# Interleaving VectorE's state rows, and taking half of the last skip terms straight from x, in a gated S5 + GELU kernel

## The chip, the cores and the metric
The kernel runs on one core of one Trainium2 chip. The metric is the device time of one execution, in microseconds; smaller is better. The kernel before has a median of 209.35 us over three runs (208.24 to 209.89).

## The reference, cut to what matters
The input x is [2048, 640] in bf16. One branch (a) is a diagonal complex state-space layer with 640 states, one is a dense layer (b) with 1728 hidden units, and a sigmoid gate per row mixes them.

```python
g = sigmoid((x * gate_w).sum(-1, keepdims=True))
Lam_bar = exp(dt * Lam)                       # complex, one per state
Bu = einsum("bld,pd->blp", x, B_bar)          # complex
h[t] = Lam_bar * h[t-1] + Bu[t]               # 2048 steps
a = 2 * einsum("blp,dp->bld", h, C).real + x * Dskip
b = gelu(x @ w1 + b1) @ w2 + b2
out = g * a + (1 - g) * b
```

## The kernel before, in words
The 2048 rows of x are cut into 4 chunks of 512 (`NCH`, `CH`), and each chunk into 4 output tiles of 128 rows (`TPC`; tile number `ti`, and `H = 2` tiles make a half). The 640 states are 5 blocks of 128 (`KS`); one block of one chunk is called a **state row** here, so there are 20.

**TensorE** runs these stages in an order written out at the end of the function (L953 to L996): `ff1(c)` (L345, matmuls L305) computes the hidden layer of a chunk, `ssm(c)` (L619, matmuls L481) computes Bu, `fin_b(c)` (L706, matmuls L717) is the second dense product by a seven-product scheme on halves, and the state part of the output is `fin_a(c)` (L784, matmuls L797) for chunks 0 and 1 and `fin_s(c)` (L845, matmuls L857, seven products again) for chunks 2 and 3. The last stages are `fin_b(2)`, `fin_s(2)`, `fin_b(3)`, `fin_s(3)`. All products are made in 8 PSUM banks of 128 x 512 f32 (`bank()`); a product into a bank that is reused waits for the last reader of that bank.

**ScalarE** evicts PSUM: the GELU (L314), Bu into a bf16 tile `bu` (L484), copies of a bank into another one (`fork`, L729 in `fin_b` and L863 in `fin_s`), and the gated outputs of the dense branch into f32 tiles `gb` (`out_of`, L737). `part_7` (L750) writes the product Q into `gq`; an accumulating DMA from GpSimd's queue (`twice`, L703; `plus`, L661) adds it, in both column halves, to another tile.

**VectorE** does the recurrence. For a state row, `scan_ops` (L546) puts nine steps in a list `pend`, each with a time from which it may run, a cost, and a function: `f1` cos product of bu, `f2` sin product of bu, `f3` their sum v (a rotation by the state's angle, so that the recurrence becomes real), `f4` twice a `tensor_tensor_scan` over 512 steps (real and imaginary part; L571), `f5` the carry to the next chunk, `f6`, `f7`, `f8` the rotation back into `hs`. All products go through one function, so that their line is L552. The tiles `wa`, `wb` and `v` have one buffer each, `g` has two, `bu` eight. For chunks 1 and 2, `f5` leaves the carry to four small ScalarE instructions (L585), which read the last column of `g`.

**The order on each engine** is the order in which the program issues instructions. A small clock model (`ck`, L225) decides it: each matmul adds to `ck.pe`, each ScalarE instruction to `ck.act`. `let_out(until)` (L236) issues steps from `pend` as long as the modelled VectorE time is before `until`; `dve_now(ready, cost, fn)` (L246) first lets steps out up to `ready` and then issues `fn`. The model knows nothing of a DMA's landing. Other VectorE work stands between the state rows in this way: the fold of C (L533), the skip products x * Dskip (`skip`, L647), the output evictions (`ot`, L802 and L872), the four sums of `hs` for the seven products (`h_sums`, L824).

**SP's queue** carries the loads and stores in program order: after the last `ff1`, two DMA transposes of `gelN` (L337), a load `gel<-eL` (L343), then the loads of x tiles (`load_xn`, L126).

**The skip term of the last two chunks.** For tiles of chunks 2 and 3, x * Dskip (bf16, `xn`) is multiplied by the gate on ScalarE into an f32 tile `GS[c][a]` (`gated`, L833, instruction L836), for all four tiles of the chunk, and VectorE adds that to `gb` (`skip_in`, L839, instruction L843, which the profile shows as L842). The f32 tiles lie in weights that are no longer used (`wide`, L818 to L820). For tiles 2 and 3 of the chunk, `fin_b` first lets the DMA (`twice(gs[H + j], ...)`) add Q into the same tile.

```python
986  fin_b(2, {1: lambda: (gated(2, H), gated(2, 0), load_xn(NT - TPC), load_xn(NT - TPC + 1)),
987            2: lambda: minus_c(3),
988            3: lambda: skip_in(2, (0, 1), 0, HD)}, GS[2])
990  fin_s(2, lhs, rhs, {0: lambda: skip_in(2, (0, 1), HD, D, ck.act + 0.5), 1: lambda: minus_d(3)})
991  skips(3, H)
992  fin_b(3, {0: lambda: (let_out(1e9), skips(3), [f() for f in last]), 1: lambda: gated(3, H), 2: lambda: gated(3, 0),
993            3: lambda: skip_in(3, (0, 1), 0, HD)}, GS[3])
```

The numbers 0 to 3 are hooks, places in `fin_b` (L753 to L779) and `fin_s`. In `fin_b` hook 1 stands behind the products into Y, hook 2 behind `out_of("X", 1, 1)`, and hook 3 behind `out_of("Z", 1, 0)`, ahead of the last product and `out_of("X", 0, 1)`. So the x tiles of chunk 3 are loaded at L981 (tiles 14 and 15, into `w1c_hi` and `xB`) and at L986 (tiles 12 and 13, into the `xn` pool), their skip products are made at L991 and L992, and they are gated in `fin_b(3)`.

Of the kernel before, what the change touches and what calls it, by code (L numbers as in the profile page):

```python
# [42 lines left out]
def kernel(  # L43
# [80 lines left out]
    def load_xn(ti, dst=None):  # L124
        xn[ti] = xnp.tile([P, D], BF16, name="xn") if dst is None else dst
        nc.sync.dma_start(out=xn[ti][:], in_=x2d[ti * P:(ti + 1) * P, :])  # L126
# [106 lines left out]
    def later(ready, cost, fn, c=-1):  # L233
        pend.append((ready, cost, fn, c))
# [307 lines left out]
    def settle(keep=None):  # L542
        while small and (ck.pe > small[0][0] if keep is None else len(small) > keep):
            small.pop(0)[1]()

    def scan_ops(c, ks, bu, ready):  # L546
        wide = lambda t: t[:, ks:ks + 1, :].to_broadcast([P, 2, CH])
        sines = TSIN2[:, ks, :, :]
        s = {}

        def tt(o, a, b, op):
            nc.vector.tensor_tensor(out=o, in0=a, in1=b, op=op)  # L552

        def f1():
            s["mc"] = work.tile([P, 2, CH], BF16, name="wa", bufs=1)
            tt(s["mc"][:], wide(TCOS), bu[:], ALU.mult)

        def f2():
            s["ms"] = work.tile([P, 2, CH], BF16, name="wb", bufs=1)
            tt(s["ms"][:], sines, bu[:], ALU.mult)  # L560

        def f3():
            s["v"] = work.tile([P, 2, CH], BF16, name="v", bufs=1)
            tt(s["v"][:], s["mc"][:], s["ms"][:, ::-1, :], ALU.add)

        def f4(ri):
# [4 lines left out]
            nc.vector.tensor_tensor_scan(s["g"][:, ri, :], r_c[:, ks:ks + 1].to_broadcast([P, CH]),  # L571
                                         s["v"][:, ri, :], init, ALU.mult, ALU.add)

        def f5():
            g = s["g"]
            if c == 0:
                m = work.tile([P, 2], F32, name="e2")
                end = g[:, :, CH - 1:CH].rearrange("p r o -> p (r o)")
                tt(m[:], end[:, ::-1], sn[:, ks, :], ALU.mult)
                nc.vector.scalar_tensor_tensor(out=carry[:, :, ks], in0=end, scalar=cL[:, ks:ks + 1], in1=m[:], op0=ALU.mult, op1=ALU.add)  # L580
                return

            def turn_carry():
                m = work.tile([P, 2], F32, name="e1")
                one = lambda out, i, sc, b: nc.scalar.activation(out=out, in_=g[:, i, CH - 1:CH], func=ACT.Identity,  # L585
                                                                 scale=sc[:, ks:ks + 1], bias=b)
# [8 lines left out]
        def f6():  # L595
            s["no"] = work.tile([P, 2, CH], BF16, name="wa", bufs=1)
            tt(s["no"][:], wide(TCOS), s["g"][:], ALU.mult)

        def f7():
            s["ns"] = work.tile([P, 2, CH], BF16, name="wb", bufs=1)  # L600
            tt(s["ns"][:], sines, s["g"][:], ALU.mult)

        def f8():
            to = lambda t: t.rearrange("p r (i t) -> p r i t", i=2)
            dst = hs[c][:].rearrange("p i r k t -> p r i k t")[:, :, :, ks, :]
            tt(dst, to(s["no"][:]), to(s["ns"][:, ::-1, :]), ALU.subtract)

        later(ready, 0.68, f1)
        later(0, 0.65, f2)
        later(0, 0.75, f3)  # L610
        later(0, 1.27, lambda: f4(0))
        later(0, 1.21, lambda: f4(1))
        if c < NCH - 1:
            later(0, 0.25 if c == 0 else 0.0, f5)
        later(0, 0.69, f6)
        later(0, 0.62, f7)
        later(0, 0.7, f8, c)

    def ssm(c, at={}, given=()):  # L619
        hs[c] = hsp.tile([P, 2, 2, KS, HT], BF16, name="hs")  # L620
# [82 lines left out]
    def twice(dst, src):  # L703
        plus(dst.rearrange("p (h d) -> p h d", h=2), src[:].rearrange("p (o d) -> p o d", o=1).to_broadcast([P, 2, HD]))

    def fin_b(c, at={}, gs=None):  # L706
# [54 lines left out]
        if c == NCH - 1:  # L761
            part_7()
            for j in range(H):
                twice(gs[H + j], gq[j])
        both("X", N2, TB)
        fork("X", "Z")
        if c < NCH - 1:
            part_7()
        if c == NCH - 2:
            for j in range(H):  # L770
                twice(gs[H + j], gq[j])
        both("X", s1, TA)
        out_of("X", 1, 1)
        hook(2)
# [43 lines left out]
    wide = [narrow(w1a_sb[:], 6 * D)[:, j * 2 * D:(j + 1) * 2 * D].bitcast(F32) for j in range(3)]  # L818
    wide += [xA[:].rearrange("p k t -> p (k t)")[:, KS * HT:].bitcast(F32), narrow(w1c_lo[:], 2 * D).bitcast(F32)]
    GS = {2: [wide[i] for i in (0, 1, 3, 4)], 3: [wide[i] for i in (2, 0, 3, 4)]}  # L820
# [12 lines left out]
    def gated(c, a0):  # L833
        for a in (a0, a0 + 1):
            ti = c * TPC + a
            nc.scalar.activation(out=GS[c][a], in_=xn[ti][:], func=ACT.Identity, scale=gcol[:, 0, ti:ti + 1])  # L836
            act(0.82)

    def skip_in(c, tiles, d0, d1, ready=0):  # L839
        for a in tiles:  # L840
            gb = gbs[c * TPC + a]
            dve_now(ready, 0.82 if d1 - d0 > HD else 0.45, lambda: nc.vector.tensor_tensor(  # L842
                out=gb[:, d0:d1], in0=gb[:, d0:d1], in1=GS[c][a][:, d0:d1], op=ALU.add))  # L843

    def fin_s(c, lhs, rhs, at={}):  # L845
        A = dict(zip((1, 7, 6, 2, 5, 3, 4), lhs))
# [103 lines left out]
    def sums(c):  # L950
# [30 lines left out]
    for j, t in ((0, w1c_hi[:].rearrange("p k f -> p (k f)")[:, 0:D]), (1, xB[:].rearrange("p k t -> p (k t)")[:, KS * HD:KS * HD + D])):  # L981
        load_xn(NT - H + j, t)
# [12 lines left out]
    skip_in(3, (0, 1), HD, D)  # L995
# [31 lines left out]
```

## Time and profile before

| what | us |
|---|---|
| median of three runs | 209.35 (208.24 to 209.89) |
| the profiled execution's own time | 207.85 |
| its span in the trace | 206.1 |
| TensorE busy | 200.8 (97%), 1290 matmuls, granted clock 1.00 |
| VectorE busy | 190.3 (92%), 304 instructions |
| ScalarE busy | 143.3 (70%), 275 instructions |
| GpSimd busy | 50.4 (24%) |
| last matmul of the chain ends | 202.06 |

Times in the trace are counted from the span's start; the execution's own time is 1.75 us more than the span. VectorE and ScalarE instructions overlap at their ends: the next one can start while the one before is still recorded as running. So the price of an instruction in a queue is the distance from its start to the next start, and not its recorded duration. The profile's releaser of a wait is the instruction that ended last among those waited for.

In the chain of work that ended last, TensorE's lines hold 91% of the span and VectorE's 6%; the VectorE part lies between 173.5 and 184.4.

### The profile page before, as it was taken

What the parts mean: (1) busy time and instruction counts of PE and PEld (TensorE: products, weight loads), DVE (VectorE), ACT (ScalarE), POOL (GpSimd) and SP (SyncE); (2) the same over time, 40 slices, a digit from 0 to 9 for tenths busy, and PEclk for the clock granted to TensorE, in tenths of its full rate; (3) what the DMA queues carried; (4) which work ended last, traced back from release to release, by engine and by line L of the source; (5) the groups of instructions that cost most, each with busy time, mean ns of one, the idle gap of its engine ahead of it and who ended that gap; (6) DMA issues with size and microseconds to landing.
All of it is one profiled execution on the core that took longest, in us unless ns stands there. A gap on an engine that the chain in (4) does not pass through costs nothing.

```text
span 206.1 us, 3584 instructions
## 1 busy us (share of the span) xinstructions
PE 200.8 (97%) x1290; PEld 120.6 (59%) x1301; DVE 190.3 (92%) x304; ACT 143.3 (70%) x275; POOL 50.4 (24%) x83
## 2 busy tenths in 40 slices
PE   8999999999999999999999999999999999998993
PEld 5844544454477644675457777544447677776762
DVE  2689998999999999999999999999999999999983
ACT  3598765997876889992574897268866987257720
POOL 8317930313230500031001052200411171014000
PEclk9999999999999999999999999999999999999999
DMA  6989998999999450269923379902676999538303
GB/s 180 206 137 229 204 275 144 199 212 264 207 147 246 109 81 11 65 113 245 197 55 60 67 133 245 238 4 80 106 133 118 167 226 202 125 94 165 61 0 127
DMA packets 45191, 30.28 MB, mean 147 GB/s; under 512 B 26899, under 2 KB 42613, under 8 KB 45173
## 3 DMA queue, kind: packets, MB, share of 16 engines
q0 software_dynamic: 6448, 12.53, 35.8%
q1 hardware_dynamic: 38148, 17.03, 34.8%
q10 hardware_dynamic: 576, 0.49, 0.8%
q8 instruction: 10, 0.16, 0.3%
q14 instruction: 9, 0.07, 0.2%
HBM read 7.79 MB, written 2.62 MB: 51 GB/s over the span
## 4 chain that ended last, share of the span: by engine, by line
PE 91%; DVE 6%; ACT 1%; issue 1%; DVEq 0%
PE bank L305 28%; PE bank L717 22%; PE bank L481 21%; PE bank L797 11%; PE bank L857 6%; DVE ot L872 2%; PE bank L264 1%; PE bank L329 1%; DVE gb L884 1%; DVE gb L842 1%; DVE wb L552 1%; PE bank L267 0%; ACT gq L750 0%; ACT xA L836 0%; ACT w1c_lo L836 0%
## 5 line engine op out<-in xcount | busy, mean ns | idle before, releaser
L314 ACT ACTIVATE gel<-bank,colB 128x512 bf16<-128x512 f32 (+1 forms) x52 | 33.5, 690 | 7.5 <-PE bank L305 7.2
L571 DVE TENSOR_TENSOR_SCAN g<-r_c,carry,v 128x512 bf16<-128x512 f32 x30 | 37.2, 1272 | 0.7
L484 ACT ACTIVATE bu<-bank 128x512 bf16<-128x512 f32 x40 | 23.2, 600 | 18.6 <-PE bank L481 18.5
L717 PEld LDWEIGHTS <-gel 128*128 128x128 bf16 x280 | 27.3, 98 | 11.8 <-issue 1.0
L717 PE MATMUL bank<-w_sb,gel 128*128 128x320 bf16 x168 | 24.1, 299 | 0.0
L305 PEld LDWEIGHTS <-w1a_sb 128*128 128x128 bf16 x162 | 14.7, 103 | 12.0
L737 ACT ACTIVATE gb<-bank,gcol 128x320 f32<-128x320 f32 x32 | 16.0, 524 | 6.5 <-PE bank L717 6.5
L797 PEld LDWEIGHTS <-hs 128*128 128x128 bf16 x160 | 15.6, 98 | 6.0
L481 PEld LDWEIGHTS <-BT_im 128*128 128x128 bf16 x100 | 9.8, 98 | 11.8
L481 PEld LDWEIGHTS <-BT_re 128*128 128x128 bf16 x100 | 9.7, 98 | 11.0
L552 DVE TENSOR_TENSOR wa<-TCOS,bu 128x1024 bf16<-128x1024 bf16 x20 | 13.7, 687 | 1.4 <-DVE hs L552 0.5
L305 PE MATMUL bank<-xA,w1a_sb 128*128 128x128 bf16 (+2 forms) x100 | 14.8, 303 | 0.1
L552 DVE TENSOR_TENSOR v<-wa,wb 128x1024 bf16<-128x1024 bf16 x20 | 13.9, 693 | 0.7
L552 DVE TENSOR_TENSOR hs<-wa,wb 128x1024 bf16<-128x1024 bf16 x20 | 13.8, 690 | 0.6
L552 DVE TENSOR_TENSOR wa<-TCOS,g 128x1024 bf16<-128x1024 bf16 x20 | 13.8, 691 | 0.4
L552 DVE TENSOR_TENSOR wb<-TSIN,bu 128x1024 bf16<-128x1024 bf16 x20 | 13.7, 684 | 0.0
L552 DVE TENSOR_TENSOR wb<-TSIN,g 128x1024 bf16<-128x1024 bf16 x20 | 13.7, 683 | 0.0
L797 PE MATMUL bank<-CT_re,hs 128*128 128x320 bf16 x80 | 13.5, 299 | 0.0
L797 PE MATMUL bank<-CT_im,hs 128*128 128x320 bf16 x80 | 13.5, 299 | 0.0
L717 PEld LDWEIGHTS <-N 128*128 128x128 bf16 x112 | 11.0, 98 | 4.3
L305 PEld LDWEIGHTS <-w1b_sb 128*128 128x128 bf16 x80 | 7.8, 98 | 9.4 <-DMA w1b_sb<-in_B_w_dram 0.2
L729 ACT ACTIVATE bank<-bank 128x320 f32<-128x320 f32 x16 | 6.7, 422 | 9.5 <-PE bank L717 9.3
(189 smaller groups left out, 399.2 us busy)
## 6 DMA issues: line engine op xcount, KB each, us to landing
out_dram<-ot SPq DMA_DIRECT2D x15, 160.0 KB, 3.3
w_sb<-in_B_w_dram SPq DMA_DIRECT2D x4, 480.0 KB, 5.7
gel<-N POOLq DMA_DIRECT2D x4, 448.0 KB, 4.8
xn<-in_A_x_dram SPq DMA_DIRECT2D x10, 160.0 KB, 3.1
N<-gel POOLq DMA_DIRECT2D x3, 448.0 KB, 5.4
gel<-gel POOLq DMA_DIRECT2D x3, 448.0 KB, 7.2
N<-N POOLq DMA_DIRECT2D x3, 448.0 KB, 6.1
gb<-gq POOLq DMA_DIRECT2D x4, 320.0 KB, 4.8
```

Of the source, the lines that this page charges most:

```text
L305: nc.tensor.matmul(p[:, t0:t1], lhsT=w, rhs=xT[c][:, kd, t0:t1], start=(kd == 0) if first is None else first, stop=(kd == last), skip_grou ...
L314: nc.scalar.activation(out=dst, in_=src, func=ACT.Gelu_apprx_tanh, bias=b1_c[p0:p1, kf:kf + 1])
L481: nc.tensor.matmul(p[:], lhsT=BT[ks >= KSA][:, kd, (ks % KSA if ks < KSA else ks - KSA) * P:][:, 0:P], rhs=xT[c][:, kd, :], start=(kd == 0 ...
L484: nc.scalar.activation(out=bu[:, ri, :], in_=p[:], func=ACT.Identity)
L552: nc.vector.tensor_tensor(out=o, in0=a, in1=b, op=op)
L571: nc.vector.tensor_tensor_scan(s["g"][:, ri, :], r_c[:, ks:ks + 1].to_broadcast([P, CH]), s["v"][:, ri, :], init, ALU.mult, ALU.add)
L717: nc.tensor.matmul(p[:, 0:HD], lhsT=lhs[:, s, j * P:(j + 1) * P], rhs=rhs[:, s, :], start=fresh and s == 0, stop=s == KH - 1, skip_group_c ...
L729: nc.scalar.activation(out=quad[j][dst][:, 0:HD], in_=quad[j][src][:, 0:HD], func=ACT.Identity)
L737: nc.scalar.activation(out=gbs[ti][:, h * HD:(h + 1) * HD], in_=quad[j][name][:, 0:HD], func=ACT.Identity, scale=gcol[:, 1, ti:ti + 1])
L797: nc.tensor.matmul(p[:, 0:d1 - d0], lhsT=hs[c][:, a // H, j // KS, j % KS, (a % H) * P:][:, 0:P], rhs=CT[:, j % KS, d0:d1], start=False, s ...
L857: nc.tensor.matmul(t[j][:, d0:d1], lhsT=A[i][:, k, j * P:(j + 1) * P], rhs=B[i][:, k, d0:d1], start=fresh and k == 0, stop=k == KS - 1, sk ...
L872: dve_now(ck.pe + 0.2, 0.54, lambda: nc.vector.scalar_tensor_tensor(out=ots[ti][:, o + d0:o + d1], in0=t[j][:, d0:d1], scalar=gcol[:, 0, t ...
```

## The change
Four edits:

1. `scan_ops` no longer appends a row's nine steps behind the last row's. If steps of the row before are still in `pend`, the new row's steps are woven in: one new step behind the old row's first scan, one behind its carry step, one behind its cos product out, one behind its sin product out, as long as the new row's data is due by the model and more than five of its steps are left. The modelled costs of the steps are changed too.
2. The sin products are made in place, into `bu` and into `g`. The cos product out goes to `wb`, the cos product in to `wa`. For chunks 1 and 2 a VectorE copy of the last column of `g` into a small tile `e3` (four buffers) comes in, and ScalarE's carry reads that.
3. For tiles 0 and 1 of chunks 2 and 3 there is no gated f32 copy any more: `skip_in` computes gate * (x * Dskip) + gb from the bf16 tile in one `scalar_tensor_tensor`. Only tiles 2 and 3 of a chunk keep the copy (`GS` has two tiles per chunk).
4. Order: all four x tiles of chunk 3 are loaded one after the other behind `ff1(3)`, tiles 12 and 13 now into `w1c_lo`. Their skip products move from behind `fin_s(2)` into `fin_b(2)` (hook 1 and hook 2), and `gated(3)` moves from `fin_b(3)` to hook 3 of `fin_b(2)`.

In VectorE's queue this gives, in the last stages: behind the sums for `xA`, the v and the sin product out of two state rows, then the skip products into `w1c_hi` and `xB`, and behind these the rest of the third, the fourth and the fifth state row of chunk 3, the skip products into `w1c_lo`, and the first evictions of `fin_s(2)`. In the kernel before, the two skip products stand behind all evictions of `fin_s(2)`, and the fifth state row behind them. TensorE's order of instructions is the same in both kernels; SP's has the same transfers in the same order, with another target for two of them.

```diff
-        later(ready, 0.68, f1)
-        later(0, 0.65, f2)
-        later(0, 0.75, f3)
-        later(0, 1.27, lambda: f4(0))
-        later(0, 1.21, lambda: f4(1))
...
+        def sin_in():
+            tt(bu[:], sines, bu[:], ALU.mult)
...
+            e = work.tile([P, 2], BF16, name="e3", bufs=4)
+            nc.vector.tensor_copy(out=e[:], in_=end)
...
+        def sin_out():
+            tt(s["g"][:], sines, s["g"][:], ALU.mult)
...
+        new = [(ready, 0.61, cos_in, -1), (0, 0.61, sin_in, -1), (0, 0.61, sum_in, -1), (0, 1.23, lambda: scan(0), -1),
+               (0, 1.21, lambda: scan(1), -1), (0, 0.3 if c == 0 else 0.1 if c < NCH - 1 else 0, ends if c < NCH - 1 else lambda: None, -1),
+               (0, 0.61, cos_out, -1), (0, 0.61, sin_out, -1), (0, 0.63, sum_out, c)]
+        old = latest.ops
+        latest.ops = new
+        left = [x for x in old if x in pend]
+        if not left:
+            pend.extend(new)
+            return
+        k = pend.index(left[0])
+        woven, rest = [], list(pend[k:])
+        t = ck.dve + sum(x[1] for x in pend[:k])
+        at = {3: 1, 5: 1, 6: 1, 7: 1}
+        queue = list(new)
+        for x in rest:
+            woven.append(x)
+            t += x[1]
+            if x in old and old.index(x) in at and queue and t > queue[0][0] - 0.1 and len(queue) > 5:
+                woven.append(queue.pop(0))
+                t += woven[-1][1]
+        pend[k:] = woven + queue
...
-                twice(gs[H + j], gq[j])
+                twice(gs[j], gq[j])
...
+    GS = {2: wide[0:2], 3: wide[2:4]}
...
+    def gated(c):
+        for j in range(H):
+            ti = c * TPC + H + j
+            nc.scalar.activation(out=GS[c][j], in_=xn[ti][:], func=ACT.Identity, scale=gcol[:, 0, ti:ti + 1])
             act(0.82)
...
+            if a >= H:
+                dve_now(ready, 0.82, lambda: nc.vector.tensor_tensor(out=gbs[ti][:], in0=gbs[ti][:], in1=GS[c][a - H], op=ALU.add))
+                continue
+            dve_now(ready, 0.88 if d1 - d0 > HD else 0.48, lambda: nc.vector.scalar_tensor_tensor(
+                out=gbs[ti][:, d0:d1], in0=xn[ti][:, d0:d1], scalar=gcol[:, 0, ti:ti + 1],
+                in1=gbs[ti][:, d0:d1], op0=ALU.mult, op1=ALU.add))
...
+    for a, t in ((H, w1c_hi[:].rearrange("p k f -> p (k f)")[:, 0:D]), (H + 1, xB[:].rearrange("p k t -> p (k t)")[:, KS * HD:KS * HD + D]),
+                 (0, lo[:, 0:D]), (1, lo[:, D:])):
+        load_xn((NCH - 1) * TPC + a, t)
...
-    fin_b(2, {1: lambda: (gated(2, H), gated(2, 0), load_xn(NT - TPC), load_xn(NT - TPC + 1)),
-              2: lambda: minus_c(3),
-              3: lambda: skip_in(2, (0, 1), 0, HD)}, GS[2])
+    fin_b(2, {1: lambda: (gated(2), skips(3, H)),
+              2: lambda: (minus_c(3), skips(3)),
+              3: lambda: (gated(3), skip_in(2, (0, 1), 0, HD))}, GS[2])
...
-    skips(3, H)
-    fin_b(3, {0: lambda: (let_out(1e9), skips(3), [f() for f in last]), 1: lambda: gated(3, H), 2: lambda: gated(3, 0),
+    fin_b(3, {0: lambda: (let_out(1e9), [f() for f in last]),
               3: lambda: skip_in(3, (0, 1), 0, HD)}, GS[3])
```

More of the change, by code (lines that the diff above doesn't have):

```diff
@@ L544, in settle @@
             small.pop(0)[1]()
+    class Row:
+        ops = ()
+    latest = Row()
     def scan_ops(c, ks, bu, ready):
@@ L552, in tt, with cos_in, sum_in, scan @@
             nc.vector.tensor_tensor(out=o, in0=a, in1=b, op=op)
[L554 to L562, printed above, removed]
+        def cos_in():
+            s["w"] = work.tile([P, 2, CH], BF16, name="wa", bufs=1)
+            tt(s["w"][:], wide(TCOS), bu[:], ALU.mult)
+        def sin_in():
+            tt(bu[:], sines, bu[:], ALU.mult)
+        def sum_in():
             s["v"] = work.tile([P, 2, CH], BF16, name="v", bufs=1)
-            tt(s["v"][:], s["mc"][:], s["ms"][:, ::-1, :], ALU.add)
-        def f4(ri):
+            tt(s["v"][:], s["w"][:], bu[:, ::-1, :], ALU.add)
+        def scan(ri):
             if ri == 0:
@@ L572, in f4, with ends @@
                                          s["v"][:, ri, :], init, ALU.mult, ALU.add)
-        def f5():
-            g = s["g"]
+        def ends():
+            end = s["g"][:, :, CH - 1:CH].rearrange("p r o -> p (r o)")
             if c == 0:
                 m = work.tile([P, 2], F32, name="e2")
-                end = g[:, :, CH - 1:CH].rearrange("p r o -> p (r o)")
                 tt(m[:], end[:, ::-1], sn[:, ks, :], ALU.mult)
@@ L581, in f5 @@
                 return
+            e = work.tile([P, 2], BF16, name="e3", bufs=4)
+            nc.vector.tensor_copy(out=e[:], in_=end)
             def turn_carry():
                 m = work.tile([P, 2], F32, name="e1")
-                one = lambda out, i, sc, b: nc.scalar.activation(out=out, in_=g[:, i, CH - 1:CH], func=ACT.Identity,
+                one = lambda out, i, sc, b: nc.scalar.activation(out=out, in_=e[:, i:i + 1], func=ACT.Identity,
                                                                  scale=sc[:, ks:ks + 1], bias=b)
@@ L593, in f5, with cos_out, sum_out @@
             small.append((ck.dve + 2.0, turn_carry))
[L595 to L603, printed above, removed]
+        def cos_out():
+            s["o"] = work.tile([P, 2, CH], BF16, name="wb", bufs=1)
+            tt(s["o"][:], wide(TCOS), s["g"][:], ALU.mult)
+        def sin_out():
+            tt(s["g"][:], sines, s["g"][:], ALU.mult)
+        def sum_out():
             to = lambda t: t.rearrange("p r (i t) -> p r i t", i=2)
             dst = hs[c][:].rearrange("p i r k t -> p r i k t")[:, :, :, ks, :]
-            tt(dst, to(s["no"][:]), to(s["ns"][:, ::-1, :]), ALU.subtract)
-        later(ready, 0.68, f1)
-        later(0, 0.65, f2)
-        later(0, 0.75, f3)
-        later(0, 1.27, lambda: f4(0))
-        later(0, 1.21, lambda: f4(1))
[L613 to L617, printed above, removed]
+            tt(dst, to(s["o"][:]), to(s["g"][:, ::-1, :]), ALU.subtract)
+        new = [(ready, 0.61, cos_in, -1), (0, 0.61, sin_in, -1), (0, 0.61, sum_in, -1), (0, 1.23, lambda: scan(0), -1),
[19 more added lines that the diff above has]
+        pend[k:] = woven + queue
     def ssm(c, at={}, given=()):
@@ L770, in fin_b @@
             for j in range(H):
-                twice(gs[H + j], gq[j])
+                twice(gs[j], gq[j])
         both("X", s1, TA)
@@ L817 @@
     M3 = narrow(xA[:], KS * HT).rearrange("p (k t) -> p k t", k=KS)
-    wide = [narrow(w1a_sb[:], 6 * D)[:, j * 2 * D:(j + 1) * 2 * D].bitcast(F32) for j in range(3)]
-    wide += [xA[:].rearrange("p k t -> p (k t)")[:, KS * HT:].bitcast(F32), narrow(w1c_lo[:], 2 * D).bitcast(F32)]
-    GS = {2: [wide[i] for i in (0, 1, 3, 4)], 3: [wide[i] for i in (2, 0, 3, 4)]}
     C11, C12, C21, C22 = (t[:, :, h * HD:(h + 1) * HD] for t in (CT_re, CT_im) for h in range(2))
@@ L831, in h_sums @@
         return steps, (a, M7, M6, b, g21, M3, d), (C11, U7, U6, C21, U5, C22, U4)
[L833 to L836, printed above, removed]
+    wide = [narrow(w1a_sb[:], 6 * D)[:, j * 2 * D:(j + 1) * 2 * D].bitcast(F32) for j in range(3)]
+    wide.append(xA[:].rearrange("p k t -> p (k t)")[:, KS * HT:].bitcast(F32))
+    GS = {2: wide[0:2], 3: wide[2:4]}
[3 more added lines that the diff above has]
+            nc.scalar.activation(out=GS[c][j], in_=xn[ti][:], func=ACT.Identity, scale=gcol[:, 0, ti:ti + 1])
             act(0.82)
@@ L840, in skip_in @@
         for a in tiles:
-            gb = gbs[c * TPC + a]
-            dve_now(ready, 0.82 if d1 - d0 > HD else 0.45, lambda: nc.vector.tensor_tensor(
-                out=gb[:, d0:d1], in0=gb[:, d0:d1], in1=GS[c][a][:, d0:d1], op=ALU.add))
+            ti = c * TPC + a
+            if a >= H:
[4 more added lines that the diff above has]
+                in1=gbs[ti][:, d0:d1], op0=ALU.mult, op1=ALU.add))
     def fin_s(c, lhs, rhs, at={}):
@@ L980 @@
                10: lambda: (nc.sync.dma_start(out=U4, in_=C21), plus(U4, U6))})
-    for j, t in ((0, w1c_hi[:].rearrange("p k f -> p (k f)")[:, 0:D]), (1, xB[:].rearrange("p k t -> p (k t)")[:, KS * HD:KS * HD + D])):
-        load_xn(NT - H + j, t)
+    lo = narrow(w1c_lo[:], 2 * D)
+    for a, t in ((H, w1c_hi[:].rearrange("p k f -> p (k f)")[:, 0:D]), (H + 1, xB[:].rearrange("p k t -> p (k t)")[:, KS * HD:KS * HD + D]),
+                 (0, lo[:, 0:D]), (1, lo[:, D:])):
+        load_xn((NCH - 1) * TPC + a, t)
     gates(3)
```

## The prediction
> **What bounds the kernel now.** I read the page first, then who waits for whom, then each engine's timeline where a wait ends last. TensorE (PE) is busy for 97% of the span at full clock, and the list of TensorE's waits has one entry behind the start:
>
> ```profile
> PE 200.8 (97%) x1290; PEld 120.6 (59%) x1301; DVE 190.3 (92%) x304; ACT 143.3 (70%) x275; POOL 50.4 (24%) x83
> ```
> ```profile
> PE bank L717 <- ACT bank L729: 0.6, 1, 0.6
> ```
>
> So VectorE (DVE), busy though it is, never holds TensorE up directly in this execution. The one hole shows in TensorE's timeline of `fin_b(3)` (columns: start, duration, engine, line):
>
> ```profile
> 178.83 3.97 PE L717 MATMUL bank<-w_sb,gel 128*128 128x320 bf16 x28
> 182.63 2.06 PE L717 MATMUL bank<-w_sb,N 128*128 128x320 bf16 x14
> 184.53 2.06 PE L717 MATMUL bank<-TB,N 128*128 128x320 bf16 x14
> 187.18 2.06 PE L717 MATMUL bank<-TA,gel 128*128 128x320 bf16 x14 [0.57 <-ACT bank L729]
> ```
>
> Fourteen matmuls take 1.90 from start to start (182.63 to 184.53), so the last line was due at 186.43 and came 0.75 late. Its cause is two steps back, in ScalarE's timeline: the copy (fork, L729) stood behind the gated skip terms, and these waited for VectorE's late skip product:
>
> ```profile
> 184.42 0.83 ACT L836 ACTIVATE xA<-w1c_hi,gcol 128x640 f32<-128x640 bf16 x1 [1.06 <-DVE w1c_hi L647]
> ```
>
> VectorE's prices are read from its timeline, start to next start:
>
> ```profile
> 119.49 2.46 DVE L571 TENSOR_TENSOR_SCAN g<-r_c,carry,v 128x512 bf16<-128x512 f32 x2
> 121.86 1.12 DVE L802 SCALAR_TENSOR_TENSOR ot<-bank,gcol,gb 128x320 bf16<-128x320 f32 x2
> ...
> 124.10 0.55 DVE L802 SCALAR_TENSOR_TENSOR ot<-bank,gcol,gb 128x320 bf16<-128x320 f32 x1
> 124.56 0.68 DVE L552 TENSOR_TENSOR hs<-wa,wb 128x1024 bf16<-128x1024 bf16 x1
> 125.16 0.55 DVE L802 SCALAR_TENSOR_TENSOR ot<-bank,gcol,gb 128x320 bf16<-128x320 f32 x1
> ...
> 163.92 0.69 DVE L552 TENSOR_TENSOR wa<-TCOS,g 128x1024 bf16<-128x1024 bf16 x1
> 164.53 0.68 DVE L552 TENSOR_TENSOR wb<-TSIN,g 128x1024 bf16<-128x1024 bf16 x1
> 165.25 0.69 DVE L552 TENSOR_TENSOR hs<-wa,wb 128x1024 bf16<-128x1024 bf16 x1
> ```
>
> A product followed by independent work takes 0.605 (163.92 to 164.53), one followed by its own reader 0.72. A scan takes 1.19 (two in 2.37), an eviction of 320 columns 0.46. The lines at 124 show that a reader two places behind its writer pays nothing: hs starts 0.46 behind the eviction, though it waits for wb in front of that. Further rows: a skip product 0.40, a plain 320-column add 0.40.
>
> The loads that the change makes urgent stand at the end of SP's queue:
>
> ```profile
> 157.18 3.51 SPq L337 DMA_TRANSPOSE gel<-gelN  x2
> 162.79 0.67 SPq L343 DMA_DIRECT2D gel<-eL  x1
> 163.56 0.54 SPq L126 DMA_DIRECT2D w1c_hi<-in_A_x_dram  x1
> 164.15 0.41 SPq L126 DMA_DIRECT2D xB<-in_A_x_dram  x1
> ```
> ```profile
> w1c_hi<-in_A_x_dram SPq DMA_DIRECT2D x1, 160.0 KB, 2.4
> xB<-in_A_x_dram SPq DMA_DIRECT2D x1, 160.0 KB, 2.3
> ```
>
> L343 waits for the transposes to land and the x tiles queue behind it. They land at 163.56 + 2.4 = 165.96 and 164.15 + 2.3 = 166.45. Nobody felt that before: the skip product read w1c_hi at 183.90.
>
> **The change, part by part.**
>
> Weaving. A row in the old order costs 6.74 (wa at 134.34 to the next wa at 141.08). Woven it is six products at 0.605 and two scans at 1.19, 6.01. Where the e3 copy comes in (ten rows), add a 0.11 wait for the scan and 0.08 for the copy: 6.20. Seventeen rows at about 0.55 are some 9 us off VectorE. On the path that is nothing: TensorE waits for no VectorE work before 178.83. The old evictions in `fin_a` keep up with TensorE, and so do the new ones, whose queue is shorter. Should the cover go, it is 9 us of VectorE.
>
> The Trainium skill speaks against this edit. "VectorE: DVE Perf Modes", section "The DRAIN you can't avoid", says the pipeline empties after every VectorE instruction whatever the semaphores, so that only fewer instructions help, not another order. The rows above (0.605 against 0.72) differ. By that rule the weave would save nothing, and VectorE would come to the w1c_hi product near 169, 9 us later than by the rows, so that the sum below would be 3 us larger.
>
> In place: an in-place bf16 product is in the trace (xn<-xn,Dbc, 483 ns for 640 elements, against 690 for 1024), so no change of price. The e3 copy lies between 0.07 (the gates' 4-element instructions, start to start) and 0.22 (L580); ten of them are 0.7 to 2.2 us, hidden under the 9. ScalarE's carry reads e3 instead of g; its one old wait for g was 0.4 and held nobody. By the sums the copies come before ScalarE asks.
>
> Skip term from x: eight additions of 320 columns get a multiply. Not in the trace from SBUF; bounds are the plain add (0.40) and the eviction's whole duration (0.55); I take 0.46, the eviction's spacing, being the same operation. ScalarE loses four gated products of 0.72. That removes the 0.75 hole, and in `fin_b(2)` another 0.17 (161.45 to 163.52 is 2.07 instead of 1.90). The four accumulating DMAs of GpSimd keep number, size and order; only targets change.
>
> Gating moved: `gated(3)` now stands on ScalarE in front of the last `out_of` of `fin_b(2)`. ScalarE ends the two Z outputs at 168.5, gates until 169.9, evicts X until 170.8, and the first two forks of `fin_s(2)` end at 171.2 and 171.6. TensorE wants them at 171.94 and 172.6. It fits by 0.7; nothing.
>
> Loads of tiles 12 and 13: third and fourth in SP's queue as before (issued at 164.66), without the waits for ScalarE (0.3 and 0.2) that reading `xn` brought. With their 3.4 us they land by 168.6; VectorE's products on them come at 171.0 by the sum below. Nothing.
>
> Skip products moved: the step that decides. They now stand behind `xA` and two products. VectorE comes there about 160.2 (its queue summed with the prices above from the second row on); it can't be earlier than 159.4, since the gates wait for ScalarE's gz at 157.2 and then 0.3 + 0.74 + 1.21 follow. The data lands at 165.96. VectorE is in order, so it stands still for nearly 6 us with three unfinished state rows and the first evictions of `fin_s(2)` queued behind. Those evictions free the bank into which `fin_b(3)` writes first. From the landing on:
>
> - skip into xB at 166.45, next start 166.85
> - 4 scans 4.76, 9 products 5.45, 2 skips 0.80, 4 half additions 1.84, two reader waits 0.22: 13.07, so the eviction starts at 179.91 and ends (0.55) at 180.46. TensorE was due at 178.83: a wait of 1.6
> - the Q product of `fin_b(3)` is due 28 matmuls (3.80) later, at 184.26. Its bank waits for the third pair of evictions: from 179.91 two evictions 0.92, hs 0.61, two evictions 0.92, add to part 7 0.92 (178.26 to 179.18 before), part 7 to eviction 0.98 (179.18 to 180.16), duration 0.55: 184.81. Another 0.55
> - Q at 184.81, X at 186.71, the TA products at 188.61, with no hole now. Before they began at 187.18: 1.43 later.
>
> Behind that nothing new is late: the sums for `fin_s(3)` start near 188 and end near 191.5, the first is read at 195.6. The tail is the same.
>
> **The sum.** 207.85 + 1.43 = 209.3 for the profiled execution, which is 1.5 below the median of the runs and below all of them. I put the step on the median: 209.35 + 1.43 = 210.8.
>
> Unknowns, with both ends: landing 2.1 (the shortest of this line) to 3.4 us (the next two x tiles), -0.2 to +1.1; the half additions -0.2 to +0.4; the queue's length: the same prices over the old queue from 172.81 to 183.90 give 10.55 for 11.09, 5% short, so up to +0.9 in 17.8 us.
>
> **Rivals.**
> - No block: the loads land by 163.6, or the queue is shorter than summed. Then only the holes go: 0.75 + 0.17, 208.4. For it: VectorE saves 9 us. Against: SP's order is unchanged, and the transposes wait for ScalarE's gelN (157.0), which TensorE sets. The gain turns to a loss from a landing at 164.5 on.
> - The landing is later still, the side of clearly slower. If the first two tiles take 3.4 us like the two behind them, they land at 166.96 and 167.55, the queue starts 1.1 later, and all that follows too: 1.43 + 1.1 = 2.5, 211.9. Slower by over 1% (2.1) from a delay of 0.66 on. For it: VectorE's moved work and GpSimd's accumulating DMAs (164.75, 165.49) meet there. Against: these DMAs lie there before too.
> - The weave doesn't do what it says and each product still costs 0.72. VectorE then comes to the skip product near 169, 3 us behind the landing: 1.43 + 3 = 4.4, 213.8. Against: the lines at 124.
>
> **How the numbers follow.** Forecast 0.55, no block 0.18, later landing 0.20, no weaving gain 0.07. About 1% is what a measurement of this kernel tells from no change, here 2.1 us. Slower by over 1%: the later landing, the weave rival less a little, 0.25. Faster by over 1% needs 2.1, and the holes are 0.92 in all: 0.03. Within: 0.72. The range reaches from the no-block case, 208.4, to 1.43 + 1.1 + 0.9 = 3.4 over the median, 212.8. The likeliest case alone is 209.9 to 211.4.
>
> **What would show it.** VectorE idle before the w1c_hi product, released by a DMA, for 5 to 6 us: the block. TensorE waiting for an ot eviction at the start of `fin_b(3)` (1.6) and before Q (0.5): its price. No wait for L729's copy in `fin_b(3)`: the removed hole. Products starting 0.605 apart in woven rows: the weave. I am wrong if the wait before w1c_hi is under 4 us, if TensorE waits on ScalarE's forks at 172, or if an eviction earlier than 178 holds TensorE.

## The result, and the profile after

The changed kernel takes 209.92 us (median of 22 runs, 209.12 to 215.5). The kernel before takes 207.91 (22 runs, 207.54 to 209.89; the three on record and 19 made beside the changed kernel). The ratio is 1.0099, 95% interval 1.0072 to 1.0127; the comparison leaves out executions that were disturbed. So the change costs about 1%, near 2 us. The two profiled executions differ by less: 209.38 against 207.85 in their own times, 207.6 against 206.1 in their spans, 1.5 us either way.

Where the 1.5 us went is read in four steps. First the page's line of busy times, and the entry for the last stages in the list of TensorE's waits (us in total, times, longest), of the changed kernel:

```profile
PE 200.6 (97%) x1290; PEld 119.7 (58%) x1301; DVE 186.6 (90%) x314; ACT 140.6 (68%) x271; POOL 51.2 (25%) x83
```
```profile
PE bank L732 <- DVE ot L892: 2.0, 2, 1.8
```

VectorE is busy for 3.7 us less and ScalarE for 2.7 less, and the time is longer all the same. The fork's wait (0.6) is gone from the list, and two waits for VectorE's evictions stand in its place. TensorE's timeline shows where (start, duration, engine, line):

```profile
180.51 4.09 PE L732 MATMUL bank<-w_sb,gel 128*128 128x320 bf16 x28 [1.76 <-DVE ot L892]
184.86 2.06 PE L732 MATMUL bank<-w_sb,N 128*128 128x320 bf16 x14 [0.26 <-DVE ot L892]
186.76 2.06 PE L732 MATMUL bank<-TB,N 128*128 128x320 bf16 x14
188.66 2.06 PE L732 MATMUL bank<-TA,gel 128*128 128x320 bf16 x14
```

The stage `fin_b(3)` begins 1.68 later than before (180.51 against 178.83), the Q product 2.23 later (184.86 against 182.63), and the TA products, with no hole in front of them now, 1.48 later (188.66 against 187.18). Behind that nothing is lost or won. What held the evictions shows in VectorE's timeline:

```profile
159.11 0.69 DVE L557 TENSOR_TENSOR g<-TSIN,g 128x1024 bf16<-128x1024 bf16 x1
165.82 0.49 DVE L662 TENSOR_TENSOR w1c_hi<-w1c_hi,Dbc 128x640 bf16<-128x640 bf16 x1 [6.03 <-DMA w1c_hi<-in_A_x_dram]
166.46 0.49 DVE L662 TENSOR_TENSOR xB<-xB,Dbc 128x640 bf16<-128x640 bf16 x1
...
179.91 1.00 DVE L892 SCALAR_TENSOR_TENSOR ot<-bank,gcol,gb 128x320 bf16<-128x320 f32 x2
...
184.26 0.55 DVE L892 SCALAR_TENSOR_TENSOR ot<-bank,gcol,gb 128x320 bf16<-128x320 f32 x1
```

VectorE comes to the skip product at 159.79 (165.82 - 6.03) and stands still for 6.03 us, for a DMA. All that is queued behind is late by that: the first eviction starts at 179.91, where the kernel before had it at 172.81. Of these 7.1 us about 6 are the wait; the rest is work that now stands in front of the eviction (without the wait it starts at 174.06, in `early_loads` below). And SP's timeline shows why the tile was late; its load is issued only when `gel<-eL` (L343) has got past the transposes:

```profile
162.71 0.67 SPq L343 DMA_DIRECT2D gel<-eL  x1
163.48 0.54 SPq L126 DMA_DIRECT2D w1c_hi<-in_A_x_dram  x1
```

### The profile page after: what moved, and what is told of

It is laid out like the page before. It is cut to its first block, busy times and chain, and to the rows that moved or that the text cites. A ratio compares the mean times of both kernels' runs of the same rounds, so it can differ in the third digit from the quotient of the medians.

```text
span 207.6 us, 3579 instructions
## 1 busy us (share of the span) xinstructions
PE 200.6 (97%) x1290; PEld 119.7 (58%) x1301; DVE 186.6 (90%) x314; ACT 140.6 (68%) x271; POOL 51.2 (25%) x83
## 4 chain that ended last, share of the span: by engine, by line
PE 85%; DVE 9%; DMA 3%; issue 1%; SPq 1%; DVEq 0%
PE bank L305 27%; PE bank L732 21%; PE bank L481 21%; PE bank L812 10%; PE bank L877 4%; DVE g L575 2%; DMA xn<-in_A_x_dram 2%; DVE ot L892 1%; PE bank L329 1%; DMA xB<-in_A_x_dram 1%; DVE hs L557 1%; DVE gb L861 1%; DVE wb L557 1%; DVE gb L904 0%; SPq L142 0%
## 5 line engine op out<-in xcount | busy, mean ns | idle before, releaser
L575 DVE TENSOR_TENSOR_SCAN g<-r_c,carry,v 128x512 bf16<-128x512 f32 x30 | 38.4, 1281 | 0.0
L305 PEld LDWEIGHTS <-w1a_sb 128*128 128x128 bf16 x162 | 14.0, 98 | 12.0
L305 PE MATMUL bank<-xA,w1a_sb 128*128 128x128 bf16 (+2 forms) x100 | 14.2, 292 | 0.1
L557 DVE TENSOR_TENSOR v<-wa,bu 128x1024 bf16<-128x1024 bf16 x20 | 13.8, 689 | 0.1
L557 DVE TENSOR_TENSOR g<-TSIN,g 128x1024 bf16<-128x1024 bf16 x20 | 13.8, 688 | 0.1
L557 DVE TENSOR_TENSOR wb<-TCOS,g 128x1024 bf16<-128x1024 bf16 x20 | 13.8, 688 | 0.0
L557 DVE TENSOR_TENSOR hs<-wb,g 128x1024 bf16<-128x1024 bf16 x20 | 13.7, 687 | 0.1
L557 DVE TENSOR_TENSOR bu<-TSIN,bu 128x1024 bf16<-128x1024 bf16 x20 | 13.7, 685 | 0.1
L305 PE MATMUL bank<-xB,w1a_sb 128*128 128x512 bf16 x59 | 13.2, 379 | 0.1
```

The source lines that it names most:

```text
L305: nc.tensor.matmul(p[:, t0:t1], lhsT=w, rhs=xT[c][:, kd, t0:t1], start=(kd == 0) if first is None else first, stop=(kd == last), skip_grou ...
```

## The experiments

The theory: the skip products of tiles 14 and 15 now stand in VectorE's queue ahead of the landing of their data; VectorE is in order, so 6 us of it are lost, and TensorE pays 2.2 of them less the hole of 0.75. The rivals: the weaving itself holds evictions back, or the late transfers cost something beside the wait. "Waits" below are those of TensorE behind 160 us in the run's profile; times are us, the lowest beside the median. Each ratio is to runs of the kernel before made beside that run, so compare ratios and not medians across rows.

| run | median | lowest | ratio to before, 95% interval | waits of TensorE |
|---|---|---|---|---|
| changed kernel | 209.92 | 209.12 | 1.0099 (1.0072 to 1.0127) | 1.76 + 0.26 |
| early_loads | 207.47 | 206.88 | 0.9941 (0.9910 to 0.9973) | none |
| late_loads | 216.44 | 214.96 | 1.0360 (1.0307 to 1.0412) | 1.95 + 3.97 |
| old_places | 208.05 | 207.46 | 1.0003 (0.9966 to 1.0041) | 0.46 |
| skip_late | 207.66 | 206.82 | 0.9983 (0.9957 to 1.0009) | none |
| weave_only | 208.45 | 207.75 | 1.0011 (0.9981 to 1.0040) | 0.51 + 0.46 |
| busy15 | 209.55 | 208.80 | 1.0068 (1.0041 to 1.0094) | 1.32 + 0.25 |
| busy20 | 211.88 | 211.39 | 1.0170 (1.0125 to 1.0216) | 3.31 + 0.24 |
| busy25 | 214.68 | 214.24 | 1.0315 (1.0262 to 1.0368) | 1.44 + 3.57 |
| no_weave | 218.76 | 215.62 | 1.0424 (1.0345 to 1.0502) | see below |
| no_weave_look | 214.35 | one run | - | 1.64 + 1.30 + 0.26 + 2.90 |
| early_no_weave | 208.37 | 207.64 | 1.0019 (0.9986 to 1.0052) | see below |
| early_no_weave_look | 208.27 | one run | - | 1.02 |

**When the data lands.** `early_loads` issues the four loads ahead of the transposes; `late_loads` turns their order.

The code cuts show the changed lines alone, shortened at `...`.

```diff
 early_loads, in the hidden layer of the last chunk, before the transposes of gelN:
+        if c == NCH - 1:
+            x_loads()        # the four load_xn of tiles 14, 15, 12, 13, which go from behind ff1(3)
         for i in range(2):
             nc.sync.dma_start_transpose(out=gel[c][:, i, KF - 1, :]
 late_loads:
-    for a, t in ((H, w1c_hi...), (H + 1, xB...), (0, lo[:, 0:D]), (1, lo[:, D:])):
+    for a, t in ((0, lo[:, 0:D]), (1, lo[:, D:]), (H, w1c_hi...), (H + 1, xB...)):
```

> The changed kernel with one thing moved: SP issues the four x tiles of chunk 3 ahead of the two transposes of gelN and not behind L343. Theory (the late landing is the whole cost): the tiles land near 158.2, VectorE stands still no more before the w1c_hi product, the first eviction of the third block of fin_b(3) starts near 173 to 174 and not at 179.9, TensorE has no wait for an ot eviction there, and the fixed holes (0.75 and 0.17) stay closed: 207.9 - 0.9 = 207.0, a ratio of 0.995 to the kernel before. Rival (the woven queue or the moved gating costs the time and the landing is beside it): the wait before w1c_hi goes, the time stays near 209.9, ratio 1.010.

Measured 207.47, ratio 0.9941. VectorE's timeline of that run:

```profile
160.21 0.48 DVE L670 TENSOR_TENSOR w1c_hi<-w1c_hi,Dbc 128x640 bf16<-128x640 bf16 x1
...
174.06 1.00 DVE L900 SCALAR_TENSOR_TENSOR ot<-bank,gcol,gb 128x320 bf16<-128x320 f32 x2
```

No bracket stands at the skip product any more, the eviction starts 5.85 sooner than in the changed kernel, and TensorE waits for nothing in these stages. As the theory said, to half a microsecond. This version is faster than both kernels, by 0.6% against the kernel before: its interval lies under 1, and the changed kernel's lies over it. The transposes paid for it: the load `gel<-eL` behind them follows at 167.09 and not at 162.71, and no wait of TensorE came of that.

> The changed kernel with the order of the four loads turned: tiles 12 and 13 first, w1c_hi and xB behind them, so that these two land about 1.0 later (two issues of about 0.5). Theory: VectorE's wait grows by 1.0, and both waits of TensorE behind it move by the same, so the time is that of the changed kernel + 1.0, near 210.9, ratio 1.015. Rival (the path runs elsewhere, and the landing is beside it): as the changed kernel, 209.9, ratio 1.010.

Measured 216.44: the direction is the theory's, the size (6.5 over the changed kernel, not 1.0) is not. SP's timeline, an entry of TensorE's list of waits, its timeline, and the row of 184 to 188 us (us, then busy us and instructions of PE, PEld, DVE, ACT and POOL, the granted clock, the DMA share and GB/s):

```profile
164.55 0.67 SPq L343 DMA_DIRECT2D gel<-eL  x1
...
166.41 0.38 SPq L126 DMA_DIRECT2D w1c_hi<-in_A_x_dram  x1
```
```profile
PE bank L877 <- ACT bank L883: 1.9, 1, 1.9
```
```profile
185.59 6.64 PE L732 MATMUL bank<-w_sb,gel 128*128 128x320 bf16 x28 [3.97 <-DVE ot L892]
192.06 2.06 PE L732 MATMUL bank<-w_sb,N 128*128 128x320 bf16 x14
```
```profile
184.00:188.00 4.00, 2.41 (x10) 1.34 (x10) 4.00 (x9) 0.35 (x1) 0.00 (x0) 0.53 0.01 5
```

Three things came together. The tile came later by 5.3 and not by 1.0 (the skip product starts at 171.14, in the changed kernel at 165.82): L343 was issued 1.84 later in this execution (the transposes started only 0.62 later), the new order added 1.09 up to the issue, and the load took 4.6 from issue to landing instead of 2.3. (The trace puts VectorE's wait there down to a product of TensorE, which the skip product doesn't read; the load's own landing, 166.41 + 4.6 = 171.0, fits the start at 171.14.) Second, ScalarE's `gated(3)`, which the change put in front of the first forks of `fin_s(2)`, waited 2.73 for the same tile, so that TensorE waited 1.95 for a fork (L883) there. Third, behind the wait of 3.97 the 28 matmuls took 6.47 (185.59 to 192.06) where the kernel before took 3.80 (178.83 to 182.63); the granted clock in 184 to 188 us was 0.53. So here lateness cost more than its own length.

**Where the instruction stands.** `old_places` undoes the order of edit 4. `skip_late` keeps the late loads and puts the skip products behind the last state row.

```diff
 both:
-    fin_b(2, {1: lambda: (gated(2), skips(3, H)),
-              2: lambda: (minus_c(3), skips(3)),
-              3: lambda: (gated(3), skip_in(2, (0, 1), 0, HD))}, GS[2])
+    fin_b(2, {1: lambda: gated(2),
+              2: lambda: minus_c(3),
+              3: lambda: skip_in(2, (0, 1), 0, HD)}, GS[2])
 old_places: skips(3, H) behind fin_s(2), skips(3) at hook 0 of fin_b(3)
 skip_late: skips(3, H), skips(3) at hook 0 of fin_s(2), behind skip_in
 both: gated(3) at hook 1 of fin_b(3)
```

> The changed kernel with the order of edit 4 undone: the skip products and the gated copies of chunk 3 stand at their old places, the weaving, the two buffers and the additions with a multiply stay. Theory: nothing on VectorE waits for the late x tiles, the skip product comes behind the rows, and the time is 0.2 to 0.9 under the kernel before, 207.0 to 207.7, ratio 0.995 to 0.999; what is left of the old hole (0.75) shows how much of it the fewer gated copies and the earlier VectorE close. Rival (the weaving is what costs): near 209.9, ratio 1.010.

Measured 208.05, ratio 1.0003: the loss is gone, so the place of edit 4 bore it. Nothing was won either, and TensorE's timeline says why:

```profile
186.75 2.06 PE L732 MATMUL bank<-TA,gel 128*128 128x320 bf16 x14 [0.46 <-ACT bank L744]
```

The old hole in front of the TA products is still 0.46 of 0.57, though two of four gated copies are gone.

> The changed kernel with its loads where they are, and the four skip products of chunk 3 put behind the last state row, just before the first evictions of fin_s(2); gated(3) goes back to its old place in fin_b(3). Theory (only the place of the waiting instruction in VectorE's queue costs): VectorE comes to the products near 172, when the tiles have been there for 5, so there is no wait for a DMA, the first eviction starts near 174.5, TensorE does not wait, and the holes of ScalarE stay closed: 207.0 to 207.4, ratio 0.993 to 0.996, as with the loads moved ahead. Rival (it was the earlier loads that gained, by something other than the wait): near the kernel before, 207.9 to 208.4, ratio 0.998 to 1.002.

Measured 207.66, ratio 0.9983. VectorE's timeline has the products at 172.39, with no wait, and the eviction behind them:

```profile
172.39 0.48 DVE L662 TENSOR_TENSOR w1c_hi<-w1c_hi,Dbc 128x640 bf16<-128x640 bf16 x1
...
174.00 1.00 DVE L892 SCALAR_TENSOR_TENSOR ot<-bank,gcol,gb 128x320 bf16<-128x320 f32 x2
```

In the profile this is what the theory asked for: TensorE waits for nothing, and the eviction starts at 174.00, as with the loads ahead (174.06). Against the changed kernel the gain is clear, the intervals are apart. Against the kernel before it is not: the interval reaches to 1.0009, and it overlaps that of `early_loads`. The ratio lies where the rival expected it (0.998 to 1.002) and not where the theory did (0.993 to 0.996), so by the times alone it isn't excluded that the early loads gained by something beside the wait. The traces speak against that: neither has a wait of TensorE there, and the profiled execution with the late loads (206.88) is not the slower one (207.54 with the early loads). Either cure takes the block away; that `early_loads` is the better of the two isn't shown.

**Late, whatever made it late.** These three are `early_loads` with extra work on VectorE behind the two skip products.

```diff
+    def stay(n):             # n = 15, 20, 25
+        x, y = xn[NT - 2][:], xn[NT - 1][:]
+        for j in range(n):
+            t = (x, y)[j % 2]
+            nc.vector.tensor_tensor(out=t, in0=t, in1=t, op=ALU.max)
-    fin_b(2, {1: lambda: (gated(2), skips(3, H)),
+    fin_b(2, {1: lambda: (gated(2), skips(3, H), stay(n)),
```

> The kernel with the loads moved ahead, and 15 extra VectorE operations (maximum of a tile with itself, which leaves its values) behind the two skip products: no wait for a DMA, and VectorE is 15 x 0.40 = 6.0 later all the same. Theory (what counts is how late VectorE's queue is, not what made it late): first eviction near 180.0 as in the changed kernel, TensorE waits 1.6 and 0.5 again, 209.0 to 209.4, ratio 1.005 to 1.008, but with runs closer together than those of the changed kernel, since no landing is on the path. Rival (contention by the transfers, or something else of the changed kernel, bears the loss): near 207.4.

Measured 209.55, ratio 1.0068, waits of 1.32 and 0.25, first eviction at 179.55. TensorE's timeline:

```profile
180.14 4.09 PE L740 MATMUL bank<-w_sb,gel 128*128 128x320 bf16 x28 [1.32 <-DVE ot L900]
```

With no wait for a DMA in VectorE's queue, 15 extra operations cost nearly what the wait for the DMA cost: waits of 1.57 against 2.02, the first eviction 0.36 sooner, and the intervals overlap. So VectorE's lateness is enough to make the loss. That the runs would lie closer together isn't settled: 208.80 to 210.81 over 9 runs in the comparison, against 209.12 to 211.98 over 19.

> As the run with 15 extra operations, with 20, so VectorE is 2.0 later again. Theory of a plain wait: TensorE waits 3.6 and 0.5, 211.0 to 211.4, ratio 1.015 to 1.018. Second theory, from the late loads (after a wait of 4.0 the granted clock was about 0.5 and 28 matmuls took 6.5 instead of 3.8): a wait of 3.6 is long enough for the same, the granted clock falls behind it, and 2 to 3 us come on top, 213 to 214.5, ratio 1.025 to 1.032.

> As the run with 20 extra operations (TensorE waited 3.3 and 0.3, and the granted clock stayed 1.00), with 25, so VectorE is 2.0 later again. Theory (a long wait of TensorE alone brings the clock down, as behind the wait of 4.0 with the late loads): TensorE waits about 5.3 at the start of fin_b(3), the granted clock falls to about half for some 5 us behind it, and the time is 213.9 + 2.7 = 216 to 217, ratio 1.038 to 1.045. Rival (the clock fell there for another reason): a plain wait, 213.5 to 214.2, ratio 1.026 to 1.030, granted clock 1.00.

TensorE's timeline of the run with 20, then of that with 25:

```profile
182.53 4.09 PE L740 MATMUL bank<-w_sb,gel 128*128 128x320 bf16 x28 [3.31 <-DVE ot L900]
```
```profile
184.58 5.32 PE L740 MATMUL bank<-w_sb,gel 128*128 128x320 bf16 x28 [3.57 <-DVE ot L900]
189.73 2.06 PE L740 MATMUL bank<-w_sb,N 128*128 128x320 bf16 x14
```

With 20 the wait is plain: 3.31, granted clock 1.00 behind it, and the group of 28 matmuls takes 4.09, as in the changed kernel. The profiled execution (211.39) is 2.4 above that of `busy15` (208.99), and so is its first eviction (181.93 against 179.55). The second theory falls for a wait of 3.3. With 25 it holds: 3.57 (after 1.44 for a fork in `fin_s(2)`, since ScalarE's gated copies wait for the extra work on the same tiles), and the 28 matmuls take 5.15 (184.58 to 189.73), 1.35 more than in the kernel before, at a granted clock of 0.58 in 184 to 188 us. The time fell between the two expectations: the clock's share was 1.35 and not 2.7, and the wait was split over two places. No late landing is in this, so the clock can fall behind a wait of TensorE whatever made VectorE late.

**What the weaving is worth.** `weave_only` is the kernel before with the new `scan_ops` alone; `no_weave` and `early_no_weave` are the changed kernel and `early_loads` with the old `scan_ops`. So they hold edits 1 and 2 together; the weaving and the in-place products were not tried apart. The first profiled executions of the last two had lost 3.5 and 3.2 us at 66 to 72 us to late copies, far from the change; their waits are read in a second execution of each (`no_weave_look`, `early_no_weave_look`).

> The kernel before with the new state rows alone (woven, sines in place, e3 copy); skip terms, gated copies and loads as before. Theory: about 9 us less of VectorE, nothing of it on the path but the late skip product, which comes some us earlier, so that ScalarE's fork is on time and the hole of 0.75 closes: 207.1 to 207.9, ratio 0.996 to 1.000, with rows near 6.0 to 6.2 long. Rival (woven rows hold evictions back): slower than before, ratio over 1.003.

Measured 208.45, ratio 1.0011: no difference. That fits neither a gain nor a loss from the weaving. (Of TensorE's two waits in this profile, the 0.46 is the old hole; the 0.51 is a fork that came late because ScalarE had waited 1.03 for an accumulating DMA to read `gq`.) VectorE's state rows do take some 7 us less (the sum is given below, under "The weaving"), and its timeline shows where they went:

```profile
177.58 1.23 DVE L887 SCALAR_TENSOR_TENSOR ot<-bank,gcol,gb 128x320 bf16<-128x320 f32 x2 [3.57 <-PE bank L872]
...
184.37 0.48 DVE L662 TENSOR_TENSOR w1c_hi<-w1c_hi,Dbc 128x640 bf16<-128x640 bf16 x1
```

VectorE is done with all state rows at 172.5, then waits 3.57 for TensorE at the second pair of evictions. The skip product stands behind the evictions, so it starts at 184.37, no sooner than before (183.90). The expectation that it would come some us earlier was wrong: an engine ahead of its time loses its lead at the first thing that it must wait for.

> The changed kernel with the old state rows, so skip terms, gated copies and places are new and nothing is woven. Theory: VectorE comes to the w1c_hi product near 160.0 and stands still until 166, as in the changed kernel, and the first eviction of fin_s(2) comes near 179.9; but the last row now lies between and behind the evictions, so that the third pair comes 1.4 later and the sums for fin_s(3) end near 198.7, 2 to 3 us after TensorE wants them: 211 to 214, ratio 1.015 to 1.030. Rival (the weaving bears a part of the loss): near or below the changed kernel, 209.0 to 209.9, ratio 1.005 to 1.010.

> The run without weaving once more, for a profile: the first one lost 3.2 at 67 to 72 us to copies that landed late (gel, TC), far from the change. Theory: without that loss VectorE still stands still for 6 or more before w1c_hi, TensorE waits about 3 and 1.3 in fin_b(3), and 2.9 again in fin_s(3) for the evictions behind the last row; 215 to 216. Rival (the waits in fin_s(3) came from the early loss): no wait in fin_s(3), 211 to 213.

> The kernel with the loads moved ahead, with the old state rows: the skip terms, gated copies and places are new, nothing is woven, nothing waits for a late tile. Theory (the weaving takes 9 us off VectorE where VectorE has room, so without the block it is worth nothing): first eviction near 174, last sum for fin_s(3) near 193.5 as in the kernel before, TensorE waits for no eviction, 207.0 to 207.5, ratio 0.994 to 0.998, as with the weaving. Rival (without the weaving VectorE is the bound, and the block only shows it): the waits of the run without weaving stay in part, 209 or more, ratio over 1.005.

> The run with early loads and old rows once more, for a profile: the first one lost 3.2 at 67 to 72 us in the same way. Theory: without that loss the wait of 1.0 in fin_s(3) for an eviction stays, since VectorE has the last row behind the evictions of fin_s(2) and then the sums and eight additions; 207.6 to 208.4. Rival (the wait came from the early loss): no wait of TensorE, 206.8 to 207.2.

TensorE's waits in the second profile of `no_weave` (214.35), then in that of `early_no_weave` (208.27), and the end of TensorE's timeline in the first profile of `no_weave` (220.85):

```profile
PE bank L867 <- DVE ot L882: 2.9, 1, 2.9
PE bank L722 <- DVE ot L882: 1.9, 2, 1.6
PE bank L722 <- ACT bank L734: 1.3, 1, 1.3
```
```profile
PE bank L875 <- DVE ot L890: 1.0, 1, 1.0
```
```profile
211.28 2.25 PE L867 MATMUL bank<-CT_im,xA 128*128 128x320 bf16 x10 [2.90 <-DVE ot L882]
213.32 2.52 PE L867 MATMUL bank<-w1b_sb,hs 128*128 128x320 bf16 x15
```

Without the weaving, the same block (5.99 before `w1c_hi`) costs TensorE 6.1 and not 2.0: the last row stands between and behind the evictions, so the later evictions and the sums for `fin_s(3)` come late too. The 214.35 is 0.35 over the first expectation and under the second; the four earlier runs (lowest 215.62) are over both ends of the first. The one of them that was profiled is 6.5 above 214.35, and the two traces account for that: 3.5 is the early loss; 1.33 is a longer wait at the start of `fin_b(3)` (2.97 against 1.64), with L343 issued 6.95 behind the start of the transposes and not 5.61; 1.67 is the clock, which was 0.50 from about 212 to 215 behind the wait of 2.90, so that the last two groups took 2.04 and 2.52 and not 1.36 and 1.53. The wait in `fin_s(3)` is 2.90 in both profiles, so it did not come from the early loss. Without the block the weaving is still worth 1.0: TensorE waits that long in `fin_s(3)` when the rows are old, and the intervals of `early_no_weave` and `early_loads` are apart. So the theory's sentence "worth nothing" is wrong for the changed arrangement, and right for the kernel before.

## Why the prediction held, and where it was off

- **What bounds the kernel.** Right: TensorE, with one hole, and VectorE's late skip product as its cause. The evidence is that the hole went where the skip product came sooner (changed kernel, `early_loads`, `skip_late`), and stood in `old_places` and `weave_only`, where it didn't.
- **The block.** Right to a few tenths. VectorE came at 159.79 (160.2 was worked out), `w1c_hi` let it go at 165.82 (165.96), the next start behind xB's product was 166.87 (166.85), the first eviction 179.91 (179.91), so 13.04 of queue against 13.07. The two delays were 1.68 and 0.55 more (1.6 and 0.55), the Q product at 184.86 (184.81), the TA products 1.48 late (1.43). Without the block the prediction had 0.92 under the kernel before; `early_loads` shows 0.6 to 1.9 (0.27% to 0.90% of 208).
- **The weaving.** Its price per product was right: they start 0.60 apart.

```profile
134.26 0.69 DVE L557 TENSOR_TENSOR wb<-TCOS,g 128x1024 bf16<-128x1024 bf16 x1
134.86 0.69 DVE L557 TENSOR_TENSOR bu<-TSIN,bu 128x1024 bf16<-128x1024 bf16 x1
```

  Each takes 0.69 and the next, which belongs to the other row, starts 0.60 behind it. The Trainium skill's page "VectorE: DVE Perf Modes", section "The DRAIN you can't avoid", says that the next instruction does not start until the pipeline is empty, and adds that one that is not held starts earlier. The prediction left the addition out; that order gains nothing is its own conclusion. The rows decide: a product with an independent neighbour behind it costs 0.60, one with its reader behind it 0.72, and the rival at 213.8 fell.

  The saving over the whole kernel was over-counted. Summed from start to next start over VectorE's whole timeline, without the waits in brackets, the steps of the state rows with their small copies take 131.2 in the kernel before and 124.0 in the changed kernel and in `weave_only`: 7.2 less, not some 9. A likely reason, not tried, is that many old rows already had evictions between their steps, as in the lines at 124 that the prediction shows. The result doesn't hang on this, since "on the path that is nothing" was right against the kernel before (`weave_only`). It was too narrow, though: the edits to the skip term lean on the weaving, by 1.0 without the block and by 4.1 (6.1 - 2.0) with it.

- **The skip term.** Right: the half additions take 0.46 (two of them and the next start in 0.92), and the hole of 0.75 is gone, as is the 0.17 in `fin_b(2)` (161.37 to 163.27 is 1.90). It isn't the fewer gated copies that closed the first, as the prediction had it: `old_places` has them and keeps 0.46. The skip product's earlier place closed it: `skip_late` gates in `fin_b(3)` as `old_places` does, has the product at 172.39 and not at 183.47, and has no hole.
- **Gating moved.** The fit of 0.7 held in the profile: the first two forks end by 171.24, and TensorE didn't wait. But the prediction called it nothing without saying that it hangs on the same landing. `late_loads` shows it: 1.95 at `fin_s(2)` when the tile comes 5 later.
- **The later landing, as a rival.** Priced at 1.0 for 1.0. That holds for small delays (`busy15` to `busy20`: 2.0 more of VectorE, 2.0 more of wait). It was too low where the waits were longer, 3.57 and 3.97: there the clock fell, and ScalarE's gating added a wait of its own.
- **The sum.** The step was right (1.43, measured 1.53 between the profiled executions) and the base was not: it was put on the median of three runs, 209.35, though the profiled execution's own 207.85 was there to be seen. Twenty-two runs, those three among them, gave 207.91. On that base the sum is 209.3, and 209.92 was measured; on the chosen one it is 210.8. That the forecast came so near owes something to luck: its base was 1.44 too high, and the medians moved 0.6 more than its step. "Within 1%", its likeliest side, held by a hair: the ratio is 1.0099, and its interval reaches to 1.0127.
- **What stays open.** Medians moved by 2.0, profiled executions by 1.5. The landing may bear the rest: SP issued L343 at 162.7 to 162.9 in the profiles of the kernel before, the changed one, `old_places` and `skip_late`, but at 164.4 in `weave_only` and 164.55 in `late_loads`, with the transposes begun within 0.8 of each other. Before the change nobody waited for that; after it every such delay is paid. Four of the changed kernel's 19 runs in the comparison had a mean granted clock of 0.990 to 0.992 (`busy25`, with its half clock, has 0.989), and no run of the kernel before in the later comparisons (62 runs) was below 0.996. That speaks for it, but it isn't the whole: three others of the 19 had a full clock (1.000) and took 210.92 to 211.46. No trace of any of these runs was taken, and `busy15`, which has the lateness without the landing, isn't told apart from the changed kernel (intervals 1.0041 to 1.0094 and 1.0072 to 1.0127).

## What to carry to other kernels

On an engine that works in order, an instruction whose data comes by DMA belongs behind the landing, not where the engine has room; look up when the load was issued and what the queue that issues it was waiting for. Moving the load ahead of that wait, or the instruction behind other work, cures it, and the room that was made elsewhere is worth something only where the path sees it. Put a computed step on the profiled execution's own time, not on a median of three.

## What the runs showed of the hardware

- TensorE's clock fell to half for a few microseconds behind some waits of TensorE and not behind others. In the four microseconds of 184 to 188 it was 0.53 on average behind a wait of 3.97, 0.58 behind 3.57, 1.00 behind 3.31; the two that fell also had a shorter wait (1.95 and 1.44) some 10 us earlier. It made 28 matmuls take 6.47 and 5.15 instead of 3.80. Behind a wait of 2.90 it fell to 0.50 in the first profile of `no_weave` and stayed at 1.00 in the second. Looked at by quarters of a microsecond, it was 0.50 from about 184.2 to 191.0 in `late_loads` and from 184.0 to 187.3 in `busy25`, and it had come down before the wait was over (at 185.59 and 184.58). The Trainium skill's page "TensorE: Matmul & The Clock Gate", section "HAM oscillation — how this bites in real kernels", gives a gap of about 3.4 us as the bound; the waits of 3.31, 3.57 and 3.97 agree with it, the 2.90 of `no_weave` doesn't, so here the length of the wait alone didn't decide.
- A pair of DMA transposes took a different time in programs whose instructions are the same up to there: from its start to the next issue of the queue that waits for it, 5.61 in the changed kernel (157.10 to 162.71) and 6.83 in `late_loads` (157.72 to 164.55); in the two profiles of `no_weave`, one and the same program, 6.95 and 5.61.
- The load of `w1c_hi` took 2.3 from issue to landing in the changed kernel and 4.6 in `late_loads`, where it was issued 2.9 later. What made the difference wasn't tried.
